# Half-sequence loads and stores, weights loaded once, and one operand ring for weight gradients in a backward pass

## The chip, the cores and the metric

The kernel runs on one core of a Trainium2 chip. The metric is the device time of one execution in microseconds (us). Most runs were of the fast state; the few slow ones are left out of the ratios.

Engines are named as the profile names them: PE is TensorE (PEld its weight loads), ACT ScalarE, DVE VectorE, POOL GpSimd, SP SyncE, which here only issues DMAs. ACTq and SPq are the instruction streams of ScalarE and SyncE in which DMA issues stand. PEclk is the granted share of the TensorE clock.

## The reference

The program is the forward and the backward pass of four residual blocks, A B A B, over a sequence of 2048 tokens of width 640 with 32 heads of 20. A is linear attention. B is causal attention with a window of 256 keys. It returns the output and the gradients of the input and of the four weight matrices.

```python
def _B_ref(x, wqkv, wo):                 # B, S, D = 1, 2048, 640; H = 32; W = 256
    qkv = (x @ wqkv).reshape(B, S, 3, H, Dh) ...
    scores = einsum("bhqd,bhkd->bhqk", q, k) * Dh ** -0.5
    mask = (idx[:, None] - idx[None, :] >= 0) & (idx[:, None] - idx[None, :] < W)
    p = softmax(where(mask, scores, -1e9))
    return (p @ v) ... @ wo
# x = x + A(ln(x)); x = x + B(ln(x)); x = x + A(ln(x)); x = x + B(ln(x))
_out, _vjp = jax.vjp(_f, A_x, A_wqkv, A_wo, B_wqkv, B_wo)
```

## The kernel before

The backward pass has these stages, in this order: a first stage that makes the gradient dO of the last B block; the attention backward of B (block 3); "B to A" and "A to B", which carry the gradient through the projections of one block into the next; the same again for block 1; and last the weight gradients.

The attention backward works on eight groups of four heads. A group has 16 steps, one for each tile of 128 queries. A step makes scores, their exponentials `e` (ScalarE), the gradient of the scores `ds` (VectorE), and its transpose `dsT`. The transpose is a DMA on SyncE's queue, issued as soon as `ds` is there and used five steps later.

```python
def seg_attention_bwd(self, l):
    units = [(g, b) for g in range(G) for b in range(TT)]      # 8 groups x 16 steps
    psl = self.pool(st, "atl", 2); pe = self.pool(st, "ate", 9)
    def load(g):                                # 7 loads of 512 KB on ScalarE's queue
        for i, n in enumerate(("QT", "KT", "VT")):
            r[n] = psl.tile([P, T], BF, name=n)
            self.dma(r[n], sv["qkvT"][:, i * G + g, :])
        r["dOT"] = ...; r["q"], r["k"], r["dO"] = ...
        out_of[g] = psl.tile([P, 3, T], BF, name="dqkvT_g")
    def store(g):                               # 12 stores of 80 KB on SyncE's queue
        for w in range(3):
            for hh in range(4):
                f0 = w * D + (4 * g + hh) * DH
                self.dma(self.dqkvT_d[l][f0:f0 + DH, :], out_of[g][HP * hh:HP * hh + DH, w, :], nc.sync)
    def dscore(u, half, ps):                    # VectorE: ds = ps * e
        ...
        if half == 1:
            self.tr(dsT_of[u][:, 0:4 * nkt, :], ds_of[u][:, 0:4 * nkt * P])    # SyncE's queue
    ...
    for s in range(n + LAG):                    # LAG = 8
        if s < n and units[s][1] == 6 and units[s][0] + 1 < G:
            load(units[s][0] + 1)               # the next group, all at once at step 6
        ...

def seg_B_to_A(self, l, acc, dqT):
    WT = self.load_w(pW, 1, "WT")               # both DMA transposes from DRAM, each time
    WoT = self.load_w(pW, 0, "WoT")
    ...

def weight_grads(self, ls, out_dW, out_dWo):    # called for layers (3, 1), then (2, 0)
    for kind, (srcs, width, dst) in enumerate(((self.hn_d, 480, out_dW), (self.o_d, HD, out_dWo))):
        with ExitStack() as s2:                 # pools of its own for each product
            lhs = [...]                         # loaded whole, then rhs by columns, two buffers
```

`self.dma` issues on ScalarE's queue unless told otherwise, `self.st` and `self.tr` (the transpose) on SyncE's, `self.ld` on GpSimd's.

The softmax here doesn't subtract the row's maximum and nothing guards it: scores larger than these inputs give would overflow.

## Time and profile before

Before the change the median was 2888.38 us (2881.89 to 2896.53, four runs beside the changed kernel). The profiled execution took 2894.6 us. The table is made from the timeline: a "mask" is the first causal mask instruction of a step on GpSimd, which marks the pace of the attention backward.

| Milestone | at us | since the one above |
|---|---|---|
| first matmul of the first dO stage | 915.0 | |
| first mask of the attention backward, block 3 | 979.2 | 64.2 |
| last mask | 1379.7 | 400.5 |
| first matmul of B to A | 1433.4 | 53.7 |
| first mask of the attention backward, block 1 | 1754.5 | 321.2 |
| last mask | 2137.2 | 382.6 |
| first matmul of B to A | 2189.9 | 52.7 |
| first weight-gradient matmul | 2473.1 | 283.2 |
| end | 2894.6 | 421.5 |

The page of the kernel before draws the span in 40 equal slices (72 us each). A digit is the busy share in tenths. PEclk is the granted clock.

```profile
PEclk9789897688876655555598995555558979898898
DMA  6699884498884999999944669999995355835624
```

The attention backward is where PEclk shows 5 and DMA shows 9: the engines that move data are busy all the time and the clock is at half. Over most of the first attention stage of the kernel before, the view of stretches gives (stretch, its length, then busy time of PE, PEld, DVE, ACT and POOL with counts, granted clock, DMA share, GB/s):

```profile
1010.00:1372.00 362.00, 274.76 (x3831) 106.06 (x3820) 220.10 (x280) 203.05 (x336) 128.31 (x210) 0.50 1.12 195
```

A DMA share over 1 means that packets overlap on an engine. So sums of packet times are not times that pass. The view of waits of the same stretch, kernel before (who waits, for what: us in total, times, the longest):

```profile
PE acc L806 <- DMA dsT<-ds: 46.9, 15, 11.7
ACT dqkvT_g L810 <- DMA dsT<-ds: 34.0, 7, 11.9
PEld L806 <- DMA dsT<-ds: 30.3, 5, 12.1
PE sp L731 <- ACT e L745: 14.3, 21, 3.8
```

TensorE waits for late transposes: 46.9 + 30.3 = 77 us, in stands (stretches in which an engine waits) of up to 12 us. One stand in the timeline of TensorE, kernel before (start, length, what; in brackets the idle time before it and what ended it), and below it SyncE's instruction stream at that moment:

```profile
1130.20 0.50 PE L731 MATMUL sp<-VT,dOT 32*128 32x384 bf16 x2
1139.11 0.51 PE L806 MATMUL acc<-dsT,ksl 128*32 128x128 bf16 x12 [8.40 <-DMA dsT<-ds]
```

```profile
1127.35 18.40 SPq L136 DMA_TRANSPOSE dsT<-ds  x4
```

Four transposes took 18.40 us to issue. Over 112 steps of this stage the issue of one transpose took 2.70 us in the mean (of the stage's step of 3.1 us), where the shortest took about 1.2 us.

Two other losses stand in the chain of work that ended last, kernel before (start, length, what):

```profile
2158.34 31.49 DMA WT_32780<-in_B_wqkv_dram
...
2453.76 18.67 DMA wg_r_36633<-dqkvT_117
2473.10 132.35 PE wg L971 x640
2605.47 0.67 DVE wg_r L975
2606.16 8.41 DMA out_dram<-wg_r
2614.73 10.24 DMA wg_r_37381<-in_grad_out_dram
2625.21 45.36 PE wg L971 x320
```

The first line is TensorE waiting for the transposed weights at the start of B to A. The others show TensorE empty before and between the products of the weight gradients, because each product has its own pools and waits for the stores of the one before.

### The profile page before, as it was taken

The numbers are of one execution on the slowest core, as the hardware profiler recorded it, in microseconds if no ns is written. First come the engines' busy times: TensorE is split into PE (matmuls) and PEld (weight loads), VectorE is DVE, ScalarE is ACT, GpSimd is POOL, SyncE is SP. The second block draws the span as 40 slices with busy tenths as digits, with TensorE's granted clock in tenths as the row PEclk, the third lists the DMA queues.
The fourth block names the chain that finished last, engine by engine and source line by source line (L and its number), as shares of the span: only waits on it lengthen the run. The fifth ranks groups of instructions, "written<-read, shape, count | busy, mean of one in ns | idle before, by whom it ended". The sixth has DMA issues, their size and how long they took to land. (4 is left out here: it accounts for less than half of the span.)

```text
span 2894.6 us, 60635 instructions
## 1 busy us (share of the span) xinstructions
PE 2261.8 (78%) x24412; PEld 1255.8 (43%) x24412; DVE 1335.5 (46%) x2804; ACT 1297.4 (45%) x2339; POOL 852.0 (29%) x1310
## 2 busy tenths in 40 slices
PE   7588997489987676778397996876866978896796
PEld 5345554245544332233265762332324756344344
DVE  6445553344324665566285675664754845000000
ACT  4257676146765555556143665654642545000000
POOL 0124444125545433333243233332442311000000
PEclk9789897688876655555598995555558979898898
DMA  6699884498884999999944669999995355835624
GB/s 199 206 173 186 176 178 126 141 182 172 178 187 119 243 210 202 178 209 180 197 153 121 165 171 227 218 205 184 226 191 164 122 137 179 197 74 188 220 73 159
DMA packets 1001434, 507.72 MB, mean 175 GB/s; under 512 B 841920, under 2 KB 964800, under 8 KB 1000128
## 3 DMA queue, kind: packets, MB, share of 16 engines
q1 hardware_dynamic: 793152, 240.60, 47.2%
q10 hardware_dynamic: 194816, 216.04, 25.3%
q0 software_dynamic: 13184, 47.20, 5.4%
q8 instruction: 191, 3.13, 0.4%
q14 instruction: 91, 0.75, 0.1%
HBM read 173.41 MB, written 148.50 MB: 111 GB/s over the span
## 5 line engine op out<-in xcount | busy, mean ns | idle before, releaser
L764 DVE TENSOR_TENSOR ds<-sp,e 128x768 bf16<-128x768 f32 (+2 forms) x512 | 460.6, 907 | 315.3 <-PE sp L731 285.3
L745 ACT ACTIVATE e<-sp 128x768 bf16<-128x768 f32 (+2 forms) x512 | 389.2, 774 | 185.8 <-PE sp L731 166.8
L359 ACT ACTIVATE e<-s 128x768 bf16<-128x768 f32 (+2 forms) x512 | 373.9, 774 | 148.0 <-PE s L357 106.6
L749 POOL TENSOR_SCALAR_AFFINE_SELECT e<-e 128x512 bf16<-128x512 bf16 x256 | 163.1, 637 | 520.0 <-ACT e L745 272.9
L731 PE MATMUL sp<-KT,QT 32*128 32x384 bf16 (+2 forms) x1024 | 243.1, 477 | 57.7 <-ACT e L745 28.9
L362 POOL TENSOR_SCALAR_AFFINE_SELECT e<-e 128x512 bf16<-128x512 bf16 x256 | 163.4, 638 | 414.1 <-ACT e L359 410.7
L731 PE MATMUL sp<-VT,dOT 32*128 32x384 bf16 (+2 forms) x1024 | 245.3, 470 | 44.9 <-DVE ds L764 28.0
L975 DVE CAST wg_r<-wg 128x480 bf16<-128x480 f32 (+1 forms) x36 | 21.7, 602 | 417.0 <-PE wg L971 417.0
L977 ACT CAST wg_r<-wg 128x480 bf16<-128x480 f32 (+1 forms) x24 | 12.4, 515 | 422.8 <-PE wg L971 403.9
L806 PE MATMUL acc<-dsT,ksl 128*32 128x128 bf16 x2880 | 125.0, 304 | 84.0 <-DMA dsT<-ds 79.7
L357 PE MATMUL s<-ring 32*128 32x128 bf16 x2880 | 168.3, 236 | 26.2 <-ACT e L359 25.0
L583 ACT ACTIVATE dh_junk<-d 128x320 bf16<-128x320 f32 x128 | 56.2, 439 | 240.1 <-PE d L581 240.0
L365 POOL TENSOR_SCALAR_AFFINE_SELECT e<-e 128x512 bf16<-128x512 bf16 x224 | 143.9, 642 | 0.0
L581 PEld LDWEIGHTS <-dqkvT 128*128 128x128 bf16 x960 | 93.1, 100 | 116.4 <-issue 81.6
L357 PEld LDWEIGHTS <-ring 32*128 32x128 bf16 x2880 | 84.2, 98 | 135.9 <-issue 128.7
L753 POOL TENSOR_SCALAR_AFFINE_SELECT e<-e 128x512 bf16<-128x512 bf16 x224 | 142.8, 637 | 0.0
L731 PEld LDWEIGHTS <-dOT 32*128 32x128 bf16 x1024 | 76.9, 99 | 149.5 <-issue 145.0
L231 PEld LDWEIGHTS <-ln_hnT 128*128 128x128 bf16 x960 | 96.5, 107 | 92.4 <-DMA ln_hnT<-ln_hn 34.6
L218 DVE TENSOR_TENSOR car<-d,car 128x320 bf16<-128x320 f32 x128 | 62.2, 486 | 158.4 <-PE d L216 157.8
L378 PEld LDWEIGHTS <-e 128*128 128x128 bf16 x2880 | 103.8, 98 | 67.1 <-POOL e L365 37.1
L806 PEld LDWEIGHTS <-ksl 128*32 128x32 bf16 x2880 | 61.9, 121 | 163.1 <-issue 112.0
L731 PEld LDWEIGHTS <-QT 32*128 32x128 bf16 x1024 | 55.0, 100 | 177.1 <-issue 174.6
(774 smaller groups left out, 4608.1 us busy)
## 6 DMA issues: line engine op xcount, KB each, us to landing
qkvT_127<-ring ACTq DMA_DIRECT2D x16, 768.0 KB
qkvT_131<-ring ACTq DMA_DIRECT2D x16, 768.0 KB
dqkvT_117<-dqkvT_g SPq DMA_DIRECT2D x96, 80.0 KB
dqkvT<-dqkvT_117 POOLq DMA_DIRECT2D x4, 1920.0 KB, 14.1
dqkvT_116<-dqkvT_g SPq DMA_DIRECT2D x96, 80.0 KB
dqkvT<-dqkvT_116 POOLq DMA_DIRECT2D x4, 1920.0 KB, 13.5
dqkv_115<-dkv_t SPq DMA_DIRECT2D x16, 320.0 KB
dqkv_114<-dkv_t SPq DMA_DIRECT2D x16, 320.0 KB
```

Of the source, the lines that this page charges most:

```text
L231: nc.tensor.matmul(ps, lhsT=hnT[:, k, :], rhs=W[:, k, ci * HD:(ci + 1) * HD], start=(k == 0), stop=(k == self.DT - 1))
L357: nc.tensor.matmul(ps[:, j, i * P:(i + 1) * P], lhsT=ring[r0:r0 + HP, G + g, kt * P:(kt + 1) * P], rhs=ring[r0:r0 + HP, g, qs], start=True ...
L359: nc.scalar.activation(ev[:, 2 * half:2 * half + 2], ps[:, :, 0:nkt * P].rearrange("p h (i q) -> p h i q", q=P), ACT.Exp, scale=self.c_att)
L362: nc.gpsimd.affine_select(out=ev[:, :, nkt - 1, :], in_=ev[:, :, nkt - 1, :], compare_op=ALU.is_ge, fill=0.0, base=0, pattern=[[0, 4], [1, ...
L365: nc.gpsimd.affine_select(out=ev[:, :, 0, :], in_=ev[:, :, 0, :], compare_op=ALU.is_ge, fill=0.0, base=-1, pattern=[[0, 4], [-1, P]], chan ...
L378: nc.tensor.matmul(ov[:, (g % 4) * 4 + hh, :], lhsT=ev[:, hh, i, :], rhs=slabs[(k0 + i) % len(slabs)][:, c0:c0 + DH + 1], start=(i == 0), ...
L731: nc.tensor.matmul(ps[:, j, 0:nkt * P], lhsT=slabs[g][ta][r0:r0 + HP, b * P:(b + 1) * P], rhs=slabs[g][tb][r0:r0 + HP, k0 * P:(k0 + nkt) * P],
L745: nc.scalar.activation(ev[:, 2 * half:2 * half + 2], ps[:, :, 0:nkt * P].rearrange("p h (i k) -> p h i k", k=P), ACT.Exp, scale=c_att)
L749: nc.gpsimd.affine_select(out=ev[:, :, nkt - 1, :], in_=ev[:, :, nkt - 1, :], compare_op=ALU.is_ge, fill=0.0, base=0, pattern=[[0, 4], [-1 ...
L753: nc.gpsimd.affine_select(out=ev[:, :, 0, :], in_=ev[:, :, 0, :], compare_op=ALU.is_ge, fill=0.0, base=-1, pattern=[[0, 4], [1, P]], chann ...
L764: nc.vector.tensor_tensor(out=dv[:, hs], in0=ps[:, :, 0:nkt * P].rearrange("p h (i k) -> p h i k", k=P), in1=ev[:, hs], op=ALU.mult)
L806: nc.tensor.matmul(acc[HP * hh:HP * (hh + 1), j * P:(j + 1) * P], lhsT=tok("k", g, k0 + i, hh), rhs=dsT[:, hh * nkt + i, :], start=(i == 0 ...
```

## The change

It has three parts. The attention backward loads and stores half sequences: seven loads of 256 KB every eight steps into three-deep slabs, and half output tiles stored as soon as they are full. The weights that both B-to-A stages need are loaded once, into a pool of their own. The weight gradients share one ring of operands, and the first operands are loaded before the stage "A to B" ahead of them.

```diff
-            psl = self.pool(st, "atl", 2)
-            pe = self.pool(st, "ate", 9)
+            psl = self.pool(st, "atl", 3)
+            po = self.pool(st, "ato", 2)
+            pe = self.pool(st, "ate")            # e: 9 buffers, ds: 8, dsT: 7
-            def load(g):
+            def load(g, h):                      # h: which half of the sequence
...
-                    r[n] = psl.tile([P, T], BF, name=n)
-                    self.dma(r[n], sv["qkvT"][:, i * G + g, :])
+                    r[n] = psl.tile([P, HT * P], BF, name=n)
+                    self.dma(r[n], sv["qkvT"][:, i * G + g, h * HT * P:(h + 1) * HT * P])
...
-            def store(g):
+            def store(g, h):                     # 24 stores of 40 KB a group instead of 12 of 80 KB
...
-                        self.dma(self.dqkvT_d[l][f0:f0 + DH, :], out_of[g][HP * hh:HP * hh + DH, w, :], nc.sync)
+                        self.dma(self.dqkvT_d[l][f0:f0 + DH, h * HT * P:(h + 1) * HT * P],
+                                 o[HP * hh:HP * hh + DH, w, :], nc.sync)
...
-                if s < n and units[s][1] == 6 and units[s][0] + 1 < G:
-                    load(units[s][0] + 1)
+                if pX is not None and s == TT:
+                    late = self.rinv[3][:, TT - 1, 0:1]
+                    self.WT_B = self.load_w(pX, 1, "WT", late)
+                    self.WoT_A = self.load_w(pX, 0, "WoT", late)
+                    if b == 2 and g > 0:
+                        load(g, 1)
+                    elif b == HT and g + 1 < G:
+                        load(g + 1, 0)
...
-            WT = self.load_w(pW, 1, "WT")
-            WoT = self.load_w(pW, 0, "WoT")
+            WT, WoT = self.WT_B, self.WoT_A
...  (weight gradients: one ring of half operands, 8 rhs and 6 lhs buffers, for all four products)
+                if l == 1:
+                    right.close()
+                    pl = self.pool(right, "wgl", 6, side="right")
+                    lhs = self.wg_lhs((3, 1), 1, pl)     # SyncE's queue, ahead of A to B
                 self.seg_A_to_B(l - 1, acc, dqT)
```

## The prediction

> **What bounds the kernel now.** Stages, from the busy table by stretches: attention backward 973-1397 and 1722-2153 us, weight gradients 2454-2894.
>
> *Attention backward.* The mask instructions in the timeline pace one step: 2.6 us when TensorE runs back to back, so 127 steps should take about 330 us. The first stage takes 400 us from first mask (979.2) to last (1379.6): about 70 us lost, in stalls of 8-14 us once per head group (near 1025, 1080, 1135, 1190, 1250, 1303). They begin after the next group's seven 512 KB loads are issued; the view of waits puts them on dsT, the transposed ds (PE 46.9 us). A group takes about 54 us against 16 x 2.6 = 41.5. The granted clock is 0.50 throughout. [...] here it stays even where PE is busy 6.5 of 6.6 us, so I expect no clock gain.
>
> *Stage starts.* The chain shows 31.5 us waiting for WT at 2158; PE stands about 40 us there and near 1393-1430.
>
> *Weight gradients.* PE L971 runs 132, 45, 132 and 46 us in the chain; between are 18.7, 8.4+10.2, 8.9+11.7 and 8.9+10.3 us of loads and output stores: about 77 us of empty PE.
>
> **What the change does.**
> 1. Half-sequence slabs, three deep: seven 256 KB loads every eight steps, and stores of half rows. Packets halve. [...] The slack between making dsT and using it, 5 steps or 13 us, did not cover a whole-group burst but should cover half. DMA stays tight: a step has a transpose of 393 KB (1.6 us at the trace's best rate, estimate)[...]. So I expect about 48 us per group, not 41.5: worth 90 us (0 to 140) in both stages. Split score matmuls cost a few us.
> 2. WT_B and WoT_A are loaded once. In instruction order they stand ahead of the first dO stage's WoT, not inside attention: 2 x 16 us saved at the B-to-A starts (then dqkvT's load and the dN memsets end last), about 9 us lost near 905-920.
> 3. Weight-gradient gaps shrink from 77 to about 10 us: first rhs 5 us, then 1-3 us per change of product: 68 us saved. Early lhs loads (5.2 MB) may cost A-to-B's start 4 us.
>
> Sum: -90 - 32 + 9 - 68 + 4 = -177 us.
>
> **Predicted: 2720 us, 8 in 10 within 2640 to 2795.** Chances: faster by over 2% 0.93, within 2% 0.06, slower 0.01.
>
> **What would show it.** Attention: groups 45-51 us apart, longest dsT wait (12 now) under 6 us, clock still 0.50. Stage starts: no WT wait in the chain, PE idle 25 us instead of 40; the dO stage starts 9 us later. Weight gradients: 365-378 us instead of 440, no out_dram wait in mid-chain.
>
> **What would make it wrong.** If stall cost goes by load bytes mixed with transposes, not by burst length, attention stays near 54 us per group and the total near 2800. If smaller packets let transposes flow freely, groups fall to 42 us and the total to 2660. If an lhs load waiting for its ring slot holds back transposes behind it on SP's queue, weight gradients keep 20 us of gaps.

Three passages are cut out of it, as marked. Two said of the hardware what no run here shows. The third held a step's DMA time for loads and stores, the total with the transpose's 1.6 us, and what mixed traffic does to it; no trace shows these figures, and measured ones stand under "The price of a transpose" near the end. No term of the forecast's own sum is cut: -90 - 32 + 9 - 68 + 4 = -177 us.

## The result, and the profile after

The changed kernel took 2803.71 us in the median (2795.72 to 2814.59, four runs). The outputs are right. The ratio to before is 0.9708, with a 95% interval of 0.966 to 0.9756. Here and below a ratio is the mean time of one kernel's fast runs over that of the other's of the same rounds, so it is not quite the ratio of the medians quoted. The direction was right. The predicted 2720 us and its range of 2640 to 2795 were missed: 85 us were gained in the median where 168 had been predicted.

The milestones of the two profiled executions (2894.6 and 2793.8 us), against the terms of the prediction:

| Stretch | before | after | change | predicted |
|---|---|---|---|---|
| before the first mask (its end moves from 979.2 to 992.2) | | | +13.0 | +9 |
| both attention stages, first to last mask | 400.5 + 382.6 | 379.2 + 374.6 | -29.3 | -90 |
| last mask to first matmul of B to A, both | 53.7 + 52.7 | 42.2 + 42.2 | -22.0 | -32 |
| first B to A and A to B | 321.2 | 325.6 | +4.4 | 0 |
| second B to A to the first weight-gradient matmul | 283.2 | 282.8 | -0.4 | } -68 + 4 |
| first weight-gradient matmul to the end | 421.5 | 355.0 | -66.5 | } |
| sum | | | -100.8 | -177 |

The attention term alone is 61 us short; the others are within 16 us of their sum. The two profiled executions differ by 101 us where the medians differ by 85, so some 16 us of this table are scatter between executions. The same two rows of the page, the changed kernel:

```profile
PEclk9788998778875855555589797555555998999999
DMA  6698886499885899999953575999998448596652
```

The clock is still at half in the attention stages and the DMA row is still full. The view of stretches and the view of waits, over the same part of the first attention stage of the changed kernel:

```profile
1015.00:1367.00 352.00, 281.35 (x4046) 111.10 (x4042) 225.88 (x287) 208.11 (x345) 131.93 (x216) 0.50 1.11 205
```

```profile
PE sp L752 <- ACT e L767: 45.8, 31, 5.7
ACT e L767 <- DMA dsT<-ds: 29.3, 6, 6.0
ACT dqkvT_g L832 <- DMA dqkvT_117<-dqkvT_g: 21.6, 5, 6.3
PE acc L828 <- DMA dsT<-ds: 10.6, 9, 1.9
```

The wait that the change aimed at has nearly gone: TensorE waits 10.6 us for late transposes instead of 77, and never longer than 1.9 us. In its place TensorE waits 45.8 us for ScalarE's exponentials (14.3 before), and ScalarE itself waits for transposes and for stores to land. ScalarE needs neither for its exponentials. It stands because it also issues the loads. It had done so before: added up from the traces, ScalarE's idle stretches of over 0.5 us that end with a load issue came to 51 and 49 us in the two stages of the kernel before, and to 54 and 51 in those of the changed kernel. The change did not shorten these stands. What is new is that TensorE waits for them, and that half of their time (27 of 54 us in the first stage) ends with the landing of a store and not of a transpose. Its timeline in the changed kernel, and below it SyncE's stream:

```profile
1101.82 0.38 ACT L812 ACTIVATE dqkvT_g<-acc 128x256 bf16<-128x256 f32 x1 [0.50 <-PE acc L807]
1107.51 0.33 ACTq L127 DMA_DIRECT2D KT<-qkvT_131  x1
1107.88 0.81 ACT L767 ACTIVATE e<-sp 128x768 bf16<-128x768 f32 x1 [5.68 <-DMA dsT<-ds]
```

```profile
1101.94 0.50 SPq L127 DMA_DIRECT2D dqkvT_117<-dqkvT_g  x1
1102.53 1.50 SPq L136 DMA_TRANSPOSE dsT<-ds  x1
1104.12 4.11 SPq L127 DMA_DIRECT2D dqkvT_117<-dqkvT_g  x8
```

ScalarE does nothing from 1102.20 to 1107.51, when it issues the load of KT. The trace tells why. Every DMA issue in it names the semaphore that it raises when it lands. All issues of the ScalarE and SyncE queues in this stage name one of eight semaphores, 101 to 108, in turn (48 or 49 issues each), and here an issue waited until the last DMA on its semaphore had landed: of 380 pairs of issues that follow one another on a semaphore, 376 have all the updates of the first between them (16 for a load or a transpose, 11 for a store), the last of them at least 16 ns before the second. The KT load's semaphore was last used by the transpose issued at 1102.53, which landed at 1107.24 to 1107.43. All 16 of ScalarE's stands of over 0.5 us before a load issue in the first stage end in this way, within 0.1 us of the landing of the DMA that used the semaphore last. In the stand above ScalarE's stream stood for 5.3 us before the issue, and its arithmetic behind it. On the eight semaphores, 54 DMAs a group (16 transposes, 24 stores, 14 loads) take turns, where before there were 35.

The weight gradients went as intended. In the chain of the changed kernel no store and no transposed weight of B to A stands any more; these are its lines from the last A to B on, to be read against those of before:

```profile
2300.03 24.05 SPq L136
...
2433.82 4.44 DMA wg_r<-in_grad_out_dram
2438.82 44.34 PE wg L1027 x304
2483.18 9.48 DMA wg_l<-hn_104
2492.71 120.47 PE wg L1027 x594
```

The 9.48 us of a load between two products look like a gap, but the chain only says what released the next matmul. TensorE's timeline of the changed kernel shows how long it was idle there:

```profile
2492.71 7.46 PE L1027 MATMUL wg<-wg_r,wg_l 128*128 128x480 bf16 x36 [1.31 <-DMA wg_l<-hn_104]
2621.59 6.69 PE L1027 MATMUL wg<-wg_r,wg_l 128*128 128x320 bf16 x48 [0.84 <-DMA wg_l<-o_107]
```

So two of the three changes of product cost 0.8 and 1.3 us, where 1 to 3 had been predicted; the third leaves no gap over 0.1 us. One gain was not predicted: the matmuls themselves took 349.5 us instead of 356.1, at a granted clock of 1.00 after the first product (0.94 to 0.98 before). The line of 24.05 us is the other side of the early loads: four lhs loads stand ahead of the next transposed weight on SyncE's queue, and that weight's issue takes 27.53 us instead of 12.39. It takes back what the first gap gained (TensorE was idle for 23.95 us there before and for 9.61 after), so this stretch stays at 283 us.

The same happens at the first dO stage. SyncE's stream and TensorE's first matmul there, the changed kernel:

```profile
900.94 15.29 SPq L136 DMA_TRANSPOSE WT_15341<-in_B_wqkv_dram  x1
916.45 5.93 SPq L136 DMA_TRANSPOSE WoT_14005<-in_B_wo_dram  x1
924.76 2.82 PE L545 MATMUL d<-WoT_14005,gT 128*128 128x320 bf16 x10 [15.67 <-DMA WoT_14005<-in_B_wo_dram]
```

In the kernel before WoT was issued at 909.26 and TensorE waited 3.98 us for it.

### The profile page after: what moved, and what is told of

Its sections match the earlier page's. It is cut to its first block, busy times and chain, and to the rows that moved or that the text cites. A ratio compares the mean times of both kernels' runs of the same rounds, so it can differ in the third digit from the quotient of the medians.

```text
span 2793.8 us, 61679 instructions
## 1 busy us (share of the span) xinstructions
PE 2253.5 (81%) x24668; PEld 1257.5 (45%) x24668; DVE 1335.0 (48%) x2804; ACT 1295.5 (46%) x2339; POOL 849.8 (30%) x1312
## 5 line engine op out<-in xcount | busy, mean ns | idle before, releaser
L366 ACT ACTIVATE e<-s 128x768 bf16<-128x768 f32 (+2 forms) x512 | 373.9, 774 | 150.7 <-PE s L364 106.3
L1027 PE MATMUL wg<-wg_r,wg_l 128*128 128x480 bf16 (+1 forms) x1920 | 349.5, 346 | 11.8 <-DMA wg_r<-in_grad_out_dram 9.6
L1027 PEld LDWEIGHTS <-wg_l 128*128 128x128 bf16 x1920 | 188.7, 98 | 172.4 <-issue 9.9
L1031 DVE CAST wg_o<-wg 128x480 bf16<-128x480 f32 (+1 forms) x36 | 21.7, 602 | 336.5 <-PE wg L1027 332.6
L588 PE MATMUL d<-WT_15341,dqkvT 128*128 128x320 bf16 x960 | 144.5, 305 | 45.9 <-DMA dqkvT<-dqkvT_116 23.0
L1033 ACT CAST wg_o<-wg 128x480 bf16<-128x480 f32 (+1 forms) x24 | 12.3, 514 | 340.2 <-PE wg L1027 340.2
```

The source lines that it names most:

```text
L366: nc.scalar.activation(ev[:, 2 * half:2 * half + 2], ps[:, :, 0:nkt * P].rearrange("p h (i q) -> p h i q", q=P), ACT.Exp, scale=self.c_att)
L588: nc.tensor.matmul(ps, lhsT=dT[k], rhs=WT[:, k, cs], start=(k == 0), stop=(k == self.QTT - 1))
L1027: nc.tensor.matmul(ps, lhsT=lhs[i][:, tt, m * P:(m + 1) * P], rhs=rhs[i][:, tt, :], start=(i == 0 and tt == 0), stop=(i == len(parts) - 1 ...
```

## The experiments

Eighteen kernels ran. The names beginning with `b` are the kernel before with something added, those with `x` the changed kernel with something altered, those with `y` and `z` candidates. The theories, in the order in which they came up:

- A: ScalarE's stands at load issues are the cost. B: the bytes and the rate of the DMA engines are. C: the issue time on SyncE's queue paces the stage. D: packets of another queue stretch the transposes (its 1.6 us for a transpose is the prediction's estimate). E, F and G are told with the last runs.

The letters in the expectations mean these. The table gives all results; "spans" are first to last mask of the two attention stages in the profiled execution. x_merge and y_gate have the same attention code and still differ by 10 and 14 us in their spans, so the timed ratio counts where they disagree.

| Kernel | median us | ratio to before, 95% | attention spans, us |
|---|---|---|---|
| before | 2878 to 2897 | | 400.5, 382.6 |
| after | 2803.71 | 0.9708, 0.966 to 0.9756 | 379.2, 374.6 |
| b_half | 2875.69 | 0.9994, 0.9954 to 1.0035 | 385.5, 374.1 |
| b_wg | 2823.56 | 0.9778, 0.9702 to 0.9854 | profile slow |
| x_pool | 2808.80 | 0.9764, 0.9721 to 0.9807 | 382.7, 386.4 |
| x_merge | 2751.04 | 0.9561, 0.9503 to 0.9618 | 360.4, 366.3 |
| x_noload (wrong result) | 2686.45 | 0.9278, 0.9245 to 0.9311 | 319.8, 321.9 |
| x_mpool | 2820.92 | 0.974, 0.9682 to 0.9799 | 388.6, 388.2 |
| x_mact | 2822.88 | 0.9751, 0.9717 to 0.9785 | 390.8, 391.1 |
| y_gate | 2742.82 | 0.9451, 0.9403 to 0.95 | 370.8, 352.1 |
| x_sp | 2826.53 | 0.9779, 0.9712 to 0.9845 | 394.4, 392.8 |
| xm_sp | 2773.79 | 0.9589, 0.9525 to 0.9654 | 373.9, 374.0 |
| b_sp | 2820.12 | 0.9756, 0.9692 to 0.9821 | 353.7, 351.5 |
| y_sp | 2767.13 | 0.9582, 0.9504 to 0.9659 | 376.1, 370.9 |
| b_sth | 2899.68 | 1.0025, 0.9961 to 1.009 | 386.6, 395.9 |
| b_lh | 2837.21 | 0.9797, 0.9719 to 0.9874 | 360.6, 355.7 |
| b_spm | 2840.07 | 0.9827, 0.9771 to 0.9882 | 359.8, 357.7 |
| z_best | 2739.30 | 0.9477, 0.9427 to 0.9528 | 358.9, 357.8 |
| b_spread | 2900.65 | 1.0056, 0.997 to 1.0142 | 390.5, 385.2 |
| b_pk | 2892.70 | 0.9968, 0.9906 to 1.0029 | 377.6, 391.4 |

### The parts alone: b_half, b_wg

b_half is the kernel before with the changed attention backward, and nothing of the weights or the weight gradients. b_wg is the kernel before with the new weight gradients and their early loads.

> The kernel before with the attention part of the change alone (half slabs, three deep; half stores). It sizes that part. From the two profiles it should be worth 29 us (first-to-last mask 400+383 to 379+375): about 2860, ratio 0.990. The blind prediction said 90 us: 2798, ratio 0.969. Both theories expect the two stalls per head group that the changed kernel shows, ended by a load issue.

> The kernel before with the weight-gradient part of the change alone (order, shared ring, early lhs loads). From the two profiles: weight gradients 441 to 360 us (-81), but A-to-B of the last pair starts 14 us later as the lhs loads stand ahead of WT's transposes: net -67, about 2821 us, ratio 0.977. If the delay of 14 us came from the other parts of the change (another memory layout) and not from the lhs loads, net -81: about 2807, ratio 0.972.

The attention part alone is worth nothing (0.9994). The weight-gradient part alone is worth 2.2%, which is 64 us of 2878, as much as predicted for it (68 less 4). The whole change is 0.9708, so about 0.6% or 18 us remain for the weights loaded once; this part was not run alone, and the figure is an estimate over different rounds, with intervals of 12 to 22 us to either side. (The profile of b_half has spans that are 23 us shorter than those of the kernel before, although its time is the same: scatter again.) So nearly all of the missing gain is missing in the attention part.

### Theory A: take the loads off ScalarE: x_pool

```diff
-                    self.dma(r[n], sv["qkvT"][...])     # ScalarE's queue
+                    self.ld(r[n], sv["qkvT"][...])      # GpSimd's queue; the same for all seven loads
```

> The changed kernel, with the attention stage's loads issued from GpSimd's queue instead of ScalarE's. Theory A (issue order): the stalls are ScalarE standing at a load whose turn to be issued has not come (ksl, KT), with the exponentials of the next step behind it in program order. Then ScalarE's gaps that end in a load issue vanish, the spans from first to last mask fall from 379 and 375 us to about 345-355 each, and the total goes from 2804 to about 2750 (ratio to before 0.952). Rival B (bandwidth): transposes and loads share saturated DMA engines and slow each other, whoever issues. Then the waits only move, to TensorE waiting for dsT; the spans stay 370-385 us and the total stays within 2790-2815 (ratio 0.967-0.975).

The wait for ScalarE went as theory A says, but the time did not. In the view of waits of x_pool, over 1015 to 1367 us:

```profile
PE acc L828 <- DMA dsT<-ds: 71.1, 23, 8.9
POOL qsl L127 <- PE acc L807: 27.7, 12, 7.6
PE sp L752 <- ACT e L767: 9.3, 28, 0.6
```

TensorE is back to waiting for late transposes. So moving the loads to GpSimd gains nothing. It does not settle theory A, though. GpSimd makes the masks, and it now stands before load issues, as ScalarE did: 77 us in each stage in stretches of over 0.5 us, of which the second line above is a part. Whether the loads would gain on a queue whose engine has nothing else to do is a rival that this run leaves; b_sp and x_sp below bear on it.

### The number of stores: x_merge, b_sth, b_lh

x_merge is the changed kernel with the three outputs of a head stored by one DMA: the same bytes and half tiles, 8 stores a group instead of 24.

```diff
-                for w in range(3):
-                    for hh in range(4):
-                        ...
+                dst = self.dqkvT_d[l].rearrange("(w f) t -> f w t", w=3)
+                for hh in range(4):
+                    f0 = (4 * g + hh) * DH
+                    self.dma(dst[f0:f0 + DH, :, h * HT * P:(h + 1) * HT * P], o[HP * hh:HP * hh + DH], nc.sync)
```

> The changed kernel, with the 12 stores of a half group merged into 4 (the three products of one head in one transfer): 8 instead of 24 store instructions per head group, the same bytes and the same row lengths. Theory A: fewer transfers stand in line ahead of a load, so ScalarE's stalls at load issues shrink by a third or more, spans about 360-365 us, total about 2770-2780. Rival B: bytes and rows are unchanged, so spans within 3 us of 379 and 375, total 2795-2810.

It gains: 0.9561 against 0.9708, with intervals that do not touch, and against 0.9764 for x_pool in the same rounds. As the bytes are the same, bytes and rate alone (theory B) do not account for it. Theory A's spans nearly came out (360 to 365 expected), and the time is better than it expected. In the view of waits of x_merge, over 1013 to 1342 us, TensorE hardly waits for ScalarE, and the waits of ScalarE for stores are not there:

```profile
PE acc L827 <- DMA dsT<-ds: 30.1, 23, 4.1
ACT e L766 <- DMA dsT<-ds: 14.5, 3, 6.6
PE sp L751 <- ACT e L766: 4.6, 9, 1.3
```

Later, two kernels did one half of the attention part each. b_sth only splits the stores of the kernel before in two; b_lh only halves the loads and keeps whole output tiles with 12 whole stores.

```diff
 b_sth:
-                        self.dma(self.dqkvT_d[l][f0:f0 + DH, :], out_of[g][HP * hh:HP * hh + DH, w, :], nc.sync)
+                        for h in range(2):
+                            cs = slice(h * (T // 2), (h + 1) * (T // 2))
+                            self.dma(self.dqkvT_d[l][f0:f0 + DH, cs], out_of[g][HP * hh:HP * hh + DH, w, cs], nc.sync)
 b_lh: b_half with
-                if b % HT == HT - 1:
-                    store(g, b // HT)
+                if b == TT - 1:
+                    store(g)                     # whole output tile, 12 whole stores
```

> The kernel before, with nothing changed but each of its 12 stores of a group split in two halves (24 issues on the sync engine's queue, the same bytes, at the same moment). Theory C (issue time on the sync engine's queue paces the attention backward): 84 more issues of about 0.45 us a stage, so both stage spans grow by 20 to 40 us (400 and 383 before) and the time is 2930 to 2965. Rival (bytes moved by the DMA engines): same bytes, so the time stays within 15 us of before.

> The kernel before, with the loads alone halved (three half slabs of each operand in flight) and the output tile and its 12 stores left whole. Theory C: the shorter transposes of the changed kernel (about 2.2 us instead of 2.6) without its 84 extra stores, so stage spans of 340 to 360 us, and a time of 2800 to 2825. Rival (halving the loads is worth nothing of itself, as the run of the attention part alone suggests): spans within 10 us of that run's 386 and 374, time 2865 to 2895.

The halved loads alone gain 2.0% (0.9797), 59 us of 2892. With halved output tiles and stores added (b_half) the gain is gone (0.9994). That is the clearest finding: the two halves of the attention part work against each other. The views of waits of b_lh (1004 to 1336 us):

```profile
PE acc L817 <- DMA dsT<-ds: 23.8, 20, 2.7
PE sp L741 <- ACT e L756: 5.7, 7, 1.9
```

and of b_half (1010 to 1360 us):

```profile
PE sp L745 <- ACT e L760: 53.0, 33, 5.2
ACT e L760 <- DMA dsT<-ds: 32.2, 7, 6.8
ACT dqkvT_g L825 <- DMA dqkvT<-dqkvT_g: 25.5, 6, 5.8
```

The wait for ScalarE comes with the halved stores on top of halved loads. b_sth missed what theory C expected: 84 more stores a stage and no time lost (1.0025). They too bring ScalarE's waits for stores, as its view of waits shows (1015 to 1367 us), but TensorE's waits for late transposes are nearly gone:

```profile
ACT dqkvT_g L792 <- DMA dqkvT<-dqkvT_g: 44.1, 6, 11.0
ACT e L747 <- DMA dqkvT<-dqkvT_g: 21.8, 6, 4.8
PE acc L808 <- DMA dsT<-ds: 1.8, 2, 1.0
```

So with whole loads the doubled stores change which wait is seen, and with halved loads they cost what these gain.

### What the loads cost at all: x_noload

```diff
-                    if b == 2 and g > 0:
-                        load(g, 1)
-                    elif b == HT and g + 1 < G:
-                        load(g + 1, 0)
+                    if b == 0 and g > 0:
+                        slabs[g, 0], slabs[g, 1] = slabs[0, 0], slabs[0, 1]     # wrong on purpose
```

> The changed kernel without the attention loads after head group 0: groups 1 to 7 reuse group 0's slabs (wrong result on purpose). Theory C (SP's queue): in the attention stage SP's queue is busy 0.91-0.96 of the time with issuing; a dsT transpose holds it 1.25 us at best but 2.1-2.7 us on average, and a store 0.45 us. If it is the loads that stretch the transposes' issue (C with contention), it falls to under 1.6 us without them, SP is busy under 0.8, steps run at TensorE's 2.6 us, spans from 379 and 375 to about 335-345, total about 2720-2735. If transposes and 24 stores fill the queue by themselves, the spans stay above 365. Theory A (ScalarE at load issues, already shaken by x_pool) expects the first as well, so this run does not tell A from C.

Without the loads of groups 1 to 7 the stages take 320 and 322 us, a step of 2.55 us. The view of stretches of x_noload:

```profile
1011.00:1304.00 293.00, 276.57 (x4038) 108.00 (x4036) 225.28 (x286) 209.66 (x344) 131.10 (x215) 0.51 0.98 166
```

TensorE is now busy for 276.57 of 293 us, and the DMA share is still 0.98. The loads cost 59 and 53 us beyond this in the changed kernel. That transposes and stores leave the DMA engines no room to hide the loads is argued from this share, and not tested. The mean issue of a transpose fell to 1.8 us, where theory C expected under 1.6, and SyncE's stream was still busy for 0.90 of the stage, where it expected under 0.8. The trace's packets, kernel before: in 112 steps of the first stage, 161,068 packets of 256 B (the transposes, 1,440 each in the mean) took 279.1 us of all 16 engines, loads 93.1 and stores 25.8, with the small rest 406 in 362 us, overlaps counted twice.

### Which queue: x_mpool, x_mact, x_sp, xm_sp, b_sp, y_sp

x_mpool and x_mact are x_merge with the stores on GpSimd's and on ScalarE's queue. x_sp, xm_sp, b_sp and y_sp are the changed kernel, x_merge, the kernel before and y_gate (below) with the loads on SyncE's queue.

```diff
 x_mpool, x_mact:
-                    self.dma(dst[...], o[...], nc.sync)
+                    self.dma(dst[...], o[...], nc.gpsimd)          # or nc.scalar
 x_sp, xm_sp, b_sp, y_sp:
-                    self.dma(r[n], ...)
+                    self.st(r[n], ...)                             # all seven loads
```

> x_merge with the merged stores issued from GpSimd's queue: SP issues nothing but transposes in the attention stage. Theory C: 16 transposes at 2.3 us are 37 us per group, below TensorE's 41.5: spans from 360 and 366 to about 345-350, SP's queue busy about 0.80-0.85, total about 2720-2735 (ratio 0.946-0.95). Rival B (the rate of the DMA engines on mixed traffic, whoever issues): bytes are the same, spans stay 357-368, SP's transposes take longer each, total 2740-2760.

> x_merge with the merged stores issued from ScalarE's queue. Theory C: as x_mpool, less what ScalarE loses by 8 issues of 0.35 us and by standing at them: spans 345-360. Rival B: no gain; spans 360-370, total 2745-2765.

> The changed kernel with the attention loads on SP's queue too, the queue of the transposes: one queue, first in first out, nothing beside it. Stores on another queue than the transposes had cost 30 us a stage (x_mpool, x_mact against x_merge), which theory C (SP's issue time) did not expect. Theory D (two queues interleaved): a transpose runs at its own rate of about 1.6 us only while no other queue feeds the same DMA engines; packets of a second queue slow both. Then spans fall from 379 and 375 to 330-345, total about 2730 (ratio 0.945). Theory C: 14 more issues of 0.4 us a group on a queue that is busy 0.92: spans 390 or more, total 2815 or more. Rival B (sum of bytes, whichever queue): spans 370-380, total 2795-2815.

> x_merge (4 stores per half group instead of 12) with the loads on SP's queue too. D: spans 325-340, 5-15 us less in total than x_sp (fewer issues), total about 2720. C: spans 375 or more. B: 360-366 as in x_merge, total 2751.

> The kernel before, whole-sequence slabs, with its loads on SP's queue and nothing else changed. D: the burst of seven 512 KB loads passes in about 10 us without transposes between, the 5 steps of slack (13 us) cover it: spans from 400 and 383 to 340-360, total about 2810 (ratio 0.972); then halving the slabs was not what the stage needed. If the burst blocks the queue for longer than the slack: spans 360-385. B or C: spans 385-410, ratio about 1.0.

The 10 us for the burst are an estimate: just before the first attention stage of the kernel before (950 to 979 us) a load's packet of 4 KB took 179 ns in the mean, and 896 of them on 16 engines come to 10.0 us.

> The candidate to beat both: y_gate with the attention loads on SP's queue. D: spans 325-340 against 371 and 352 in y_gate, total about 2690-2700 (ratio 0.93-0.935). B: as y_gate, 0.945. C: 0.955 or more.

Fewer issues on SyncE's queue did not help when the stores went elsewhere: x_mpool and x_mact are slower than x_merge (spans of 388 to 391 us against 360 and 366). In x_mpool the issue of a transpose took 2.89 us in the mean, in x_merge 2.34. The loads on SyncE's queue gave shorter transposes in every case (2.0 to 2.1 us; in b_sp 2.05 and 2.07 in the two stages, from 2.70 and 2.46 before), but theory D's spans came in b_sp alone (354 and 352). b_sp is the smallest edit of all, three words in the kernel before, and it gains 2.4%, about as much as the halved loads. It also takes ScalarE's stands away and puts no arithmetic behind the loads, which is what theory A asked for; the run does not tell this from the shorter transposes. With halved loads the same move gained nothing: x_sp and xm_sp are not faster than the changed kernel and x_merge, and y_sp (0.9582) is slower than y_gate (0.9451). x_sp and xm_sp differ in the merged stores only, and there the number of issues counted: 54 a group gave spans of 394 and 393, 38 gave 374. So two more queues for the stores gave nothing. SyncE's stream was busy issuing for 0.89 to 0.95 of the stage in nearly all kernels (about 0.85 in b_pk and 0.75 in x_mact). These issue times are not all work of the issuer, as the same transposes issue faster when no loads run (1.8 us in the mean in x_noload, 2.2 and 2.1 in the two stages of the changed kernel); how much of them is waiting was not measured.

Moving half the transposes to a second queue was not tried.

### Is it the count of issues? b_spm and z_best

b_spm is b_sp with merged whole stores (4 a group). z_best is y_gate (below) with b_spm's attention backward, and 7 instead of 9 buffers of `ds` and `dsT` so that it fits.

> The kernel before, whole slabs and whole output, with the loads on the sync engine's queue and the stores of the three outputs of a head merged (4 issues a group instead of 12). Theory C: 16 transposes at 2.05, 4 stores at about 0.8 and 6 loads at 0.65 us make 40 us a group, so stage spans of 320 to 340 us against 354 and 352 with the loads moved alone; time 2765 to 2800. Rival (something else than the issues paces the stage once the loads are on that queue): spans stay at 350, time 2810 to 2825.

> The candidate: the gated version (weights of the next stage in five pieces during the stage before the attention, loads of the weight gradients paced) with the whole slabs and whole output of the kernel before, loads on the sync engine's queue, stores merged to 4 a group, two buffers fewer of two work tiles. Theory C: stage spans of 320 to 340 us instead of the 371 and 352 of the gated version, so a time of 2680 to 2725. If the issues don't add up like this it stays at 2740 to 2770, as with halved loads on that queue.

Both missed. b_spm has 27 issues a group where b_sp has 35 and is no faster (0.9827 against 0.9756, not of the same rounds). A merged store took 1.16 us to issue where three single ones took 3 x 0.49, and the transposes rose from 2.05 to 2.22 us. So a count of issues times a fixed price (theory C) does not predict the stage.

### Burst, packet size or buffers? b_spread and b_pk

b_spread takes away the burst of the kernel before: the seven whole loads are issued one every second step. b_pk keeps the burst and halves the packets: each whole load is issued as two halves, one after the other. Theory E says that the DMA engines simply have no slack; F that smaller packets help the transposes; G that the finer buffers do.

```diff
 b_spread:
-                if s < n and units[s][1] == 6 and units[s][0] + 1 < G:
-                    load(units[s][0] + 1)
+                if s < n and units[s][1] % 2 == 1 and units[s][1] > 2 and units[s][0] + 1 < G:
+                    load(units[s][0] + 1, units[s][1] // 2 - 1)        # one of the seven
 b_pk:
-                    self.dma(r[n], sv["qkvT"][:, i * G + g, :])
+                    for h in range(2):
+                        cs = slice(h * HT * P, (h + 1) * HT * P)
+                        self.dma(r[n][:, cs], sv["qkvT"][:, i * G + g, cs])   # the same for all seven
```

> The kernel before, with the same seven whole 512 KB loads of the next group issued one every second step (steps 3, 5, ... 15) instead of all at step 6; nothing else changed, same bytes, same number of issues, same queues. The prediction's theory (the burst overruns the slack between making and using the transposed ds, the bytes themselves fit): without a burst the groups come down to 42 to 44 us, stage spans of 330 to 345 us, time 2770 to 2800. Theory E (the DMA engines have no slack: the packet times of transposes, loads and stores add up to about 1.1 times the span in every kernel with loads, whatever the order): groups stay at 46 us or more as in the best kernels so far (354 to 361 us), so spans of 350 to 385 us and a time of 2810 to 2870. Issue time on the sync engine's queue alone (theory C), already contradicted by the doubled stores that cost nothing: spans as before, 400 and 383.

> The kernel before, with each of the seven loads of a group issued as two halves one right after the other at the same step 6 into the same whole slabs (two buffers): the burst, the bytes, the buffers and the moment stay, only the packets are 2 KB instead of 4 KB (and the scalar engine issues 14 loads a group, as in the halved version). Theory F (what the halved loads gained is the smaller packet, behind which the 256-byte packets of the transposes wait less): stage spans of 355 to 370 us as with the loads alone halved (361 and 356), time 2830 to 2855. Rival G (the gain came from the finer buffers, which let a load start earlier and the stage run ahead): spans stay at 385 to 400, time 2880 to 2900.

b_spread gained nothing (1.0056): without its burst the stage is no faster. Its view of waits over the whole first stage (976 to 1366 us) shows:

```profile
ACT dqkvT_g L810 <- DMA dsT<-ds: 45.4, 5, 11.4
PE acc L806 <- DMA dsT<-ds: 37.2, 17, 6.2
PEld L806 <- DMA dsT<-ds: 7.7, 4, 3.3
```

So the burst did make transposes late: without it TensorE's waits for them fell from 77 to 45 us, the longest from 12 to 6.2, as the prediction's mechanism says. But the time did not follow. It is not a clean test, because ScalarE's stands at load issues stayed (57 and 48 us in the two stages, 51 and 49 before). b_pk gained nothing either (0.9968). Its transposes were shorter to issue (2.16 and 2.30 us against 2.70 and 2.46), as theory F expects, but TensorE waited 33.4 us for ScalarE, with its 14 load issues a group (14.3 in the kernel before). So the gain of b_lh is not that of the packets alone; whether it is the finer buffers (theory G) was not tested by itself.

### The candidate: y_gate

y_gate is x_merge with two gates. The transposed weights come in five pieces and WoT after them, each behind a step of the first dO stage, so that they stand ahead of nothing urgent. The four early lhs loads are spread over the last A to B in the same way.

```diff
+                if 5 <= i < 11:                     # in the first dO stage
+                    c, late = i - 5, self.do_slabs[(i - 1) % 5][:, 0:1]
+                    if c < 5:
+                        self.after(self.WT_B[:, 3 * c, 0:1], late)
+                        self.tr(self.WT_B[:, 3 * c:3 * c + 3, :], self.Wqkv[1][:, 3 * c * P:(3 * c + 3) * P])
+                    else: ...                       # WoT_A in the same way
...
+                        if i in (2, 4, 6, 8):       # in the last A to B
+                            self.after(t[:, 0, 0:1], self.car[:, i - 1, 0:1])
+                            self.st(t, self.o_d[ll][:, ts, :])
```

> x_merge with the two new delays of the change taken away: WT_B and WoT_A are transposed in five pieces and one in the middle of the first dO stage, behind its own WoT; the four early lhs loads are issued one by one inside the last A-to-B, behind WT_A. If the delays came from that order: first B_do matmul back from 922-925 to about 915 us, first mask 8-12 us earlier; from the first dh matmul of the last pair to the first weight-gradient matmul 282 to about 269 us; total about 2728 (ratio 0.948). If they came from memory layout, no change: 2751.

It is, with z_best, the fastest kernel: 2742.82 us, 0.9451, which beats both kernels; its median is 8 us below that of x_merge. Its first dO matmul is back at 914.9 us, but the stage then takes 73.9 us instead of 67.5, so that gate won little. The gated lhs loads shortened the stretch before the weight gradients from 282.4 to 276.2 us against x_merge's profile. z_best (0.9477) is the same within the intervals.

## Why the prediction was wrong

- **Direction and clock: right.** The kernel is faster by 2.9%, and the granted clock stayed at 0.50 in the attention stages. The prediction expected no clock gain because half clock stays here where TensorE is busy (6.56 of 6.6 us at 0.50 from 1006.6 us on, kernel before). The runs agree: x_noload has TensorE busy for 276.57 of 293 us at 0.51, and no gap between its matmuls there is longer than 2.1 us (busy time in a profile is modelled).
- **Weight gradients: right, in the sum partly by luck.** Predicted -68 and +4. b_wg alone measured 2.2%, 64 us; the profiles show -66.9 for both stretches. TensorE's gaps shrank by 74 us (60 between products, 14 before the first), where 68 was predicted, and the mechanism is the one told. The early loads cost A to B 14 us instead of 4; gaps that shrank by 6 us more than predicted and matmuls that took 7 us less, which nobody predicted, made up for it.
- **Weights loaded once: nearly right.** Predicted -32 and +9. The profiles show -22.0 and +13.0. TensorE's idle time before B to A fell from 40.4 and 40.8 us to 23.0 in both (25 predicted), and the load of dqkvT ends last there, as told.
- **Attention backward: wrong, and this is the step that failed.** The prediction said "I expect about 48 us per group, not 41.5: worth 90 us (0 to 140) in both stages". The profiles show -29.3, and the attention part alone measured 0.9994. Three things were wrong in that step.
  - The size of what there was to gain. The 54 us a group were read from the stands of the first stage and taken for all 16 groups. The first group of a stage has no late transposes yet (39.6 and 37.8 us), the last loads nothing for a next one (38.7 us for its 15 steps in both stages), and the middle groups took 53.7 us in the first stage but 51.0 in the second. After the change they take 50.7 and 50.0.
  - The stores. They entered as "stores of half rows", and their number not at all. Halving them doubled their number, and b_lh (-2.0%) against b_half (0.0%) shows that this took back the whole gain of the halved loads. x_merge, with the same bytes in a third of the stores, gets 0.9561 where the changed kernel has 0.9708.
  - The signature. "Longest dsT wait under 6 us" came true for TensorE (1.9 us), and yet the time did not come. The wait had turned into another: TensorE for ScalarE, 14.3 to 45.8 us, because ScalarE stood at load issues until transposes and stores on the same semaphore had landed. These stands are not in the prediction at all, although they were there before (51 and 49 us) and stayed (54 and 51).
- **The price of a transpose.** The prediction gave a step's transpose 1.6 us of the DMA engines, an estimate (393 KB at 243 GB/s, the fastest slice of the page before). Transposes that were issued back to back landed 2.3 us apart in the median in the kernel before, and 1.8 us in x_noload beside nothing but stores. With 1.8 to 2.3 us for it, and 0.83 and 0.23 us for loads and stores (their packet times of 93.1 and 25.8 us over 112 steps of the kernel before, overlaps counted twice), a step comes to 2.9 us or more by this estimate, against TensorE's 2.6: it has no slack.
- **The prediction's own doubt was the better guess.** "If stall cost goes by load bytes mixed with transposes, not by burst length, attention stays near 54 us per group and the total near 2800." The total is 2804; b_spread found nothing to gain from taking the burst away, and x_noload found 59 and 53 us in the loads' being there. The groups did come down, to about 50 us, and other stages gave most of the gain, so that the total came to lie at 2800 is in part chance.

What stays open: why doubled stores cost nothing with whole loads (b_sth) and all of the gain with halved ones; why halved loads gain if neither spread loads nor halved packets do; and why merged stores gain with halved loads (x_merge, xm_sp) and not with whole loads on SyncE's queue (b_spm). No single price, of bytes, of issues or of packets, fits all runs. One quantity goes with most of the spans, though no run tested it by itself: ScalarE's stands at load issues. They come to 18 to 29 us a stage in b_lh, x_merge and y_gate (spans of 352 to 371 us), and to 48 to 88 us in the kernel before, the changed kernel, b_half, b_sth, b_spread and b_pk (374 to 400). x_mpool and x_mact, with the stores on another queue, do not fit (32 to 45 us, spans of 388 to 391). What the runs show is that most of these stands end with the landing of a transpose or a store, and that they move between TensorE, ScalarE and GpSimd as issues are moved.

## What to carry to other kernels

When a DMA queue also carries the transposes that the next step needs, count the issues on it and not only the bytes, and try it: halving loads paid 2% here, halving stores at the same time lost it again, and merging stores won it back, but with the loads on that queue and whole slabs merging gained nothing (b_spm). Do not issue loads from an engine whose arithmetic is on the critical path without looking for idle time that ends with a load issue (51 and 49 us in the two stages here), and when you find such a stand, check before moving the loads that the DMA it waits for isn't late for everybody else too (in x_pool TensorE waited 71.1 us for late transposes). Take a gain per group from the difference of the stage's whole span, not from the spacing of its worst stands.
